# A spectral and dense layer stack on one core: rows turned through memory by SyncE, filter ordering on VectorE, evacuations assigned by phase

## The chip, the cores and the metric

The kernel runs on one core of a Trainium2 chip. The engines of a core that matter here are TensorE (PE, matrix products, with its weight loads shown apart as PEld), VectorE (DVE), ScalarE (ACT), GpSimd (POOL) and SyncE (SP). Each works through its own instructions in order, and they wait for one another by semaphores. SP, POOL and ACT also issue DMAs; a DMA waits on the engine that issues it, so whatever stands behind it on that engine waits too. Matrix products land in PSUM, eight banks of 128 partitions, from which DVE or ACT must carry them to the on-chip memory ("evacuate" them); the kernel hands out the banks in four pairs, in turn.

The metric is the device time of one execution in microseconds (us). A number such as L549 is a line of the kernel before.

## The reference

Four layers in a row on x of 2048 rows and 1024 columns, in bfloat16: twice a spectral layer A and a dense layer B.

```python
def _A_ref(x, w_r, w_i):
    X = rfft2(x.astype(float32), axes=(-2, -1))
    X = X * (w_r + 1j * w_i)
    return irfft2(X, s=(S, D), axes=(-2, -1)).astype(bfloat16)

def _B_ref(x, w1, b1, w2):
    h = einsum("bsd,df->bsf", x, w1) + b1
    sp = log1p(exp(-abs(h))) + where(h > 0, h, 0)
    return einsum("bsf,fd->bsd", h * tanh(sp), w2)

x = x + _A_ref(_layernorm(x), A_w_r, A_w_i)
x = x + _B_ref(_layernorm(x), B_w1, B_b1, B_w2)
x = x + _A_ref(_layernorm(x), A_w_r, A_w_i)
x = x + _B_ref(_layernorm(x), B_w1, B_b1, B_w2)
```

F, the hidden width of B, is 3584.

## The kernel before

**Layer A.** The two-dimensional transform and its inverse are products with tables of cosines and sines, in five stages. The first, `s1`, is a short transform along 16 row blocks and 8 column blocks: 128 products of a 128x128 slice of XR (x in another order) with a small matrix, eight of them to a PSUM pair, sixteen pairs j. In the first layer A the normalisation is folded into that small matrix: `scaled(j)` makes eight scaled copies MN of the table M0 (128x128 each), shared out among POOL, DVE and ACT, and `s1` asks for them four pairs ahead. In the second layer A the input is normalised already, one fixed M serves for all, and no copies are made.

The rest is cut into eight groups g and run as a software pipeline of twelve steps in `layer_A`: in step k, two halves each, `s2` of group k (L642), in the first layer A also `filter_bins` of group k (L834), `s3` of group k-1 (L680 to L683), `i1` of group k-3 (L709), `i2` of group k-4 (L730, L748). Each has its evacuation: L670 or L672 for `s2`, L687 for `s3`, L716 for `i1`, L756 or L758 for `i2`. After `s3` DVE multiplies by the complex filter WT with four instructions (L691 to L698). `filter_bins` brings the filter into the order of the bins: TensorE mirrors a part of it (L834), ACT writes that part (L848), and four plain copies with a stride of eight elements move the rest (L842, L845), on POOL in the first layer A. `keep_filter` does the same once more during the first layer B, with the copies on DVE, and stores the ordered filter in memory (`w_scratch`), from where the second layer A loads it.

**The turn.** The result U of a group has 16 rows of interest, each spread over 128 partitions, and the last product `i4` (L875) needs them turned: UT with row and group on the partitions. `row` moves one such row with one DMA from on-chip memory to on-chip memory, 128 pieces of 256 bytes into one partition. For groups 0 to 5 rows 0 to 7 go that way, all issued by SP; rows 8 to 15 go through memory, a write to `u_scratch` issued by SP and, a step later, `u_back` issued by POOL. Of groups 6 and 7 all rows go by `row`, on SP, POOL and ACT. `i4` waits for the whole of UT, and so does everything in layer B.

**Layer B.** Products with W1 (L930), Mish on ACT (L934), products with W2 (L948), added to x by DVE (L953). The weights stream in on SP.

The order on each engine is the order in which the program's methods are called; there is no scheduler. Two places matter beyond that. `constants` is called before `s1`, and in it POOL converts a small bias table (L399), which waits for the last of a row of loads that SP issues. And `u_turn` has a small table that names the queue of each row of groups 6 and 7.

Of the kernel before, what the change touches and what calls it, by code (L numbers as in the profile page):

```python
# [6 lines left out]
ALU = mybir.AluOpType  # L7
P = 128
BF = dt.bfloat16
# [165 lines left out]
class KB:  # L175
# [120 lines left out]
    def build(self):  # L296
# [5 lines left out]
        self.u_d = nc.dram_tensor("u_scratch", (8, P, 8, P), BF, kind="Internal").ap()  # L302
# [237 lines left out]
    def scaled(self, j):  # L540
        rt = self.RT
        rc = rt.ap.rearrange("p a b -> p (a b)")
        for q in range(8):
            n = 8 * j + q
            if q % 4 == 1:
                self.op(self.act, lambda e, n=n: e.activation(self.MN.ap[:, n, :], self.M0.ap, ACT.Copy, scale=rc[:, n:n + 1]),
                        reads=[rt.res, self.M0.res], parts=[self.r_mn[j]])
            else:
                self.op(self.pool if q % 8 in (2, 4, 7) else self.dve, lambda e, n=n: e.tensor_scalar(self.MN.ap[:, n, :], self.M0.ap, rc[:, n:n + 1], None, op0=ALU.mult),  # L549
                        reads=[rt.res, self.M0.res], parts=[self.r_mn[j]])  # L550

    def s1(self, li):
# [60 lines left out]
    def layer_A(self, li):  # L613
# [20 lines left out]
        def s2(g, half):  # L634

            ps, banks, _ = self.pair()
            y = self.Y.ap
            at = lambda r: y[:, r * 8 + g, :]
            fns = []

            def mm(dst, r, t, start, stop):
                fns.append(lambda e: e.matmul(dst, at(r), FD[:, t:t + dst.shape[-1] * 2], start=start, stop=stop))  # L642
            for i in range(2):
                d = ps[:, i * 512:(i + 1) * 512].rearrange("p (r k) -> p r k", r=2)
                if half == 0:
                    for kd in range(2):
                        for c in range(2):
                            mm(d[:, :, kd * P:(kd + 1) * P], 4 * kd + 2 * c + i, kd * 512 + c * 256, c == 0, c == 1)
                    continue
                for c in range(2):  # L650
                    mm(d[:, :, 0:P], 8 + 4 * c + i, 1024 + c * 256, c == 0, c == 1)
                for kd in range(2):
                    dd = d[:, :, P + kd * 64:P + kd * 64 + 64]
                    r, t = 10 + 4 * kd, (3 + kd) * 512
                    if g == 0:
                        mm(dd, r + i, t, True, True)
                    else:
                        for c in range(2):
                            mm(dd, r + c, t + c * 256 + i * P, c == 0, c == 1)
            self.group(fns, reads=[self.Y.res, self.r_fd], writes=banks)  # L660
            za, zb = zslot(g, 0), zslot(g, 1)

            zz = self.ARENA[:, o["Z"] // 2 + (2 * g % 6) * K:o["Z"] // 2 + (2 * g % 6 + 2) * K].rearrange(
                "p (s r k) -> p s r k", s=2, r=2)
            if half == 0:
                za.res.begin()
                zb.res.begin()
            dst, src = zz[:, :, :, 256 * half:256 * half + 256], ps.rearrange("p (s r k) -> p s r k", s=2, r=2)
            if half == 0:
                self.op(act, lambda e: e.activation(dst, src, ACT.Copy), reads=banks, parts=[za.res, zb.res])  # L670
            else:
                self.op(dve, lambda e: e.tensor_copy(dst, src), reads=banks, parts=[za.res, zb.res])  # L672
# [45 lines left out]
        def i2(g, half):  # L718
# [33 lines left out]
            if half == 0:  # L752
                u.res.begin()
            dst = u.ap[:, 8 * half:8 * half + 8, :].rearrange("p a b -> p (a b)")
            if half == 0 and g % 2 == 0:
                self.op(dve, lambda e: e.tensor_copy(dst, ps), reads=banks, parts=[u.res])  # L756
            else:
                self.op(act, lambda e: e.activation(dst, ps, ACT.Copy), reads=banks, parts=[u.res])  # L758
# [6 lines left out]
        def u_turn(g, half):  # L765

            u = U[g % 3]
            if half and g < 6:
                self.dma(sp, self.u_d[g], u.ap[:, 8:16, :], f"uw{g % 3}", reads=[u.res], writes=[self.r_ud[g]])
                return  # L770
            order = {6: (sp, pool), 7: ((sp, pool, sp, pool, sp, pool, sp, pool), (act, sp, act, act, sp, act, sp, act))}
            who = order[g][half] if g in order else sp
            for i in range(8):
                row(who[i] if isinstance(who, tuple) else who, g, 8 * half + i)
# [50 lines left out]
    def filter_bins(self, g, ps, banks, wr, wts, jt, r_jt, eng):  # L825

        fns = []
        for i in range(2):
            src, j0 = (i, (2, 0)[i]) if g == 0 else (1 - i, 0)
            for c in range(2):  # L830
                for kd in (1, 2, 3):
# [2 lines left out]
                    fns.append(lambda e, col=col, j=(j0 + c) * P, mov=mov: e.matmul(  # L834
                        ps[:, col:col + 64], jt[:, j:j + P], mov, start=True, stop=True))
        self.group(fns, reads=[wr.res, r_jt], writes=banks)
        for i in range(2):
            wt = wts[i]
            wt.res.begin()
            d3 = wt.ap[:, :, 0:384].rearrange("p c (k i) -> p c k i", i=P)  # L840
            lo = wr.ap[:, :, i, :].rearrange("p c (i k) -> p c k i", k=8)
            self.op(eng, lambda e, d3=d3, lo=lo: e.tensor_copy(d3[:, :, :, 0:64], lo[:, :, 0:3, :]),  # L842
                    reads=[wr.res], parts=[wt.res])
            dd = wt.ap[:, :, 384:512].rearrange("p c (k i) -> p c k i", i=64)
            self.op(eng, lambda e, dd=dd, lo=lo: e.tensor_copy(dd, lo[:, :, 3:8:4, :]),  # L845
                    reads=[wr.res], parts=[wt.res])
            src = ps[:, 512 * i:512 * i + 384].rearrange("p (c k i) -> p c k i", c=2, i=64)
            self.op(self.act, lambda e, d3=d3, src=src: e.activation(d3[:, :, :, 64:128], src, ACT.Copy),  # L848
                    reads=banks, parts=[wt.res])

    def keep_filter(self, g):

# [8 lines left out]
        self.filter_bins(g, self.PS[:, 6:8, :].rearrange("p a b -> p (a b)"), self.r_bank[6:8], wr, ws, jt.ap, jt.res, self.dve)  # L861
# [237 lines left out]
```

## Time and profile before

| What | us |
|---|---|
| Median of three runs (1150.26 to 1158.82) | 1154.47 |
| The profiled execution, of which all lines here are | 1154.65 |
| its span in the trace | 1152.8 |
| TensorE busy / DVE / ACT / POOL | 986.0 / 377.2 / 335.1 / 149.0 |
| first layer A: start to first product of `s2` | 0 to 80.72 |
| first layer A: the pipeline, to the end of the last evacuation | 80.72 to 166.39 |
| wait for UT until `i4` | 166.39 to 185.53 |
| first layer B until `s1` of the second layer A | 185.53 to 634.75 |
| second layer A: `s1` and pipeline, to the last evacuation | 634.75 to 712.34 |
| wait for UT until `i4` | 712.34 to 730.30 |
| second layer B | 730.30 to 1152.8 |

The rows of a profile are read so. In a timeline a row has its start, its length, the engine, the line, what is written from what, the shape and how often; brackets hold the engine's idle time just before and what ended it. In the groups by line, after the bar: the busy time, the mean ns of one, and the idle time before them with what ended it. In the table by stretch of time each engine has its busy time and its count, then the granted TensorE clock (1.00 is full speed), the share of the DMA engines and GB/s. The chain of waits goes back from the last instruction to whatever released it, and so shows what the end hung on; "issue" in it is time in which the engine waited for nothing that the profile names. The layers B, 870 us of the span, are TensorE work almost without gaps; the change concerns the two layers A and a part of `filter_bins` that runs within layer B.

### The profile page before, as it was taken

Reading aid. Unit: us, or ns where it says so; the run is one execution under the profiler, and the core shown is the slowest. Engines: PE = TensorE matmul, PEld = TensorE weight load, DVE = VectorE, ACT = ScalarE, POOL = GpSimd, SP = SyncE. Lnnn points to the kernel's source line nnn. Section 1 sums busy time; section 2 is a strip of 40 time slices with the busy share of each in tenths; the row PEclk is TensorE's granted clock in tenths of the full one; section 3 lists DMA queues with packets and bytes.
Section 4 is the critical chain, followed back from the end, with each engine's and each line's share of the span. In section 5 each row is a group of like instructions: output and inputs, shape, how many; then the busy total and the mean of one; then the engine's idle time right before and its main releaser. Section 6 shows DMA issues by size and latency. Waiting matters only on the chain.

```text
span 1152.8 us, 14555 instructions
## 1 busy us (share of the span) xinstructions
PE 986.0 (86%) x6090; PEld 522.3 (45%) x6185; DVE 377.2 (33%) x795; ACT 335.1 (29%) x466; POOL 149.0 (13%) x219
## 2 busy tenths in 40 slices
PE   0167973899999999999995795499999999999998
PEld 0145753444444445544442674344444444444443
DVE  6158844551044421102442783555101110000011
ACT  6045762434300024430000685243320003432000
POOL 1287531000000002200031022100000000000000
PEclk9999995999999999999998998599999999999999
DMA  9503567144400015522095057614440002210000
GB/s 282 122 4 106 123 128 152 38 151 160 147 19 19 19 55 183 183 91 74 23 116 72 29 165 135 134 48 136 146 147 19 28 19 62 76 55 1 28 19 28
DMA packets 128449, 101.97 MB, mean 88 GB/s; under 512 B 48000, under 2 KB 105600, under 8 KB 128384
## 3 DMA queue, kind: packets, MB, share of 16 engines
q1 hardware_dynamic: 114832, 69.37, 21.5%
q0 software_dynamic: 11680, 31.25, 11.8%
q10 hardware_dynamic: 1872, 0.43, 0.5%
q8 instruction: 49, 0.80, 0.3%
q14 instruction: 16, 0.13, 0.0%
HBM read 79.93 MB, written 15.47 MB: 83 GB/s over the span
## 4 chain that ended last, share of the span: by engine, by line
PE 70%; DVE 9%; DMA 8%; issue 5%; POOL 4%; ACT 3%; SPq 1%; ACTq 0%; POOLq 0%; DVEq 0%
PE PS L948 33%; PE PS L930 28%; DMA ARENA<-in_A_w_i_dram 3%; POOL ARENA L549 2%; DMA u_scratch<-ARENA 2%; DMA ARENA<-ARENA 2%; POOL ARENA L242 1%; PE PS L642 1%; DVE BN L431 1%; PE PS L912 1%; DVE XS L881 1%; PE PS L834 1%; DMA XS<-in_A_x_dram 1%; PE PS L709 1%; PE PS L730 1%
## 5 line engine op out<-in xcount | busy, mean ns | idle before, releaser
L930 PE MATMUL PS<-ARENA 128*128 128x512 bf16 x1750 | 389.3, 381 | 5.8 <-DVE ARENA L917 2.2
L948 PE MATMUL PS<-ARENA 128*128 128x512 bf16 x1754 | 387.4, 379 | 2.0
L934 ACT ACTIVATE ARENA<-PS,B 128x512 bf16<-128x512 f32 x224 | 153.8, 688 | 438.6 <-PE PS L930 438.5
L930 PEld LDWEIGHTS PS<-ARENA 128*128 128x128 bf16 x1792 | 175.5, 98 | 213.0 <-issue 4.5
L948 PEld LDWEIGHTS PS<-ARENA 128*128 128x128 bf16 x1792 | 174.7, 98 | 207.6
L953 DVE TENSOR_TENSOR XS<-PS,XS 128x512 bf16<-128x512 f32 x64 | 44.3, 692 | 502.3 <-PE PS L948 502.3
L431 DVE BATCH_NORM_STATS2 BN<-XS 128x6 f32<-128x512 bf16 x108 | 69.6, 674 | 7.6 <-DMA XS<-in_A_x_dram 6.4
L875 PE MATMUL PS<-MT,ARENA 128*128 128x32 bf16 (+1 forms) x768 | 24.5, 187 | 47.9 <-DMA ARENA<-ARENA 39.6
L881 DVE TENSOR_TENSOR XS<-PS,XS 128x512 bf16<-128x512 f32 (+1 forms) x40 | 29.1, 790 | 96.1 <-PE PS L875 96.1
L570 ACT ACTIVATE ARENA<-PS 128x1024 bf16<-128x1024 f32 x16 | 16.3, 1024 | 149.8 <-PE PS L564 149.5
L564 PE MATMUL PS<-ARENA 128*128 128x128 bf16 x128 | 16.2, 306 | 38.4 <-POOL ARENA L549 33.5
L875 PEld LDWEIGHTS PS<-MT,ARENA 128*128 128x128 bf16 x768 | 22.9, 100 | 51.4 <-issue 44.7
L687 ACT ACTIVATE ARENA<-PS 128x1024 bf16<-128x1024 f32 x32 | 32.7, 1023 | 25.8 <-PE PS L683 25.8
L412 ACT ACTIVATE ARENA<-XS 128x1024 bf16<-128x1024 bf16 x20 | 21.1, 1056 | 59.5 <-DVE XS L881 48.5
L642 PE MATMUL PS<-FD,ARENA 128*128 128x256 bf16 (+1 forms) x312 | 35.5, 266 | 2.7 <-DVE ARENA L572 1.2
L709 PE MATMUL PS<-ARENA 128*128 128x256 bf16 x256 | 34.1, 277 | 2.3 <-DMA ARENA<-c_bt 2.3
L242 POOL DMA_DIRECT2D w_scratch<-ARENA x8 | 4.6, 576 | 230.9 <-ACT ARENA L848 230.9
L572 DVE CAST ARENA<-PS 128x1024 bf16<-128x1024 f32 x16 | 19.1, 1222 | 45.4 <-PE PS L564 45.4
L716 ACT ACTIVATE ARENA<-PS 128x1024 bf16<-128x1024 f32 x32 | 32.6, 1020 | 4.4 <-PE PS L709 4.4
L642 PEld LDWEIGHTS PS<-FD,ARENA 128*128 128x128 bf16 x312 | 27.6, 103 | 9.3 <-issue 1.9
L691 DVE TENSOR_TENSOR ARENA<-ARENA 128x1024 bf16<-128x1024 bf16 x32 | 25.4, 794 | 18.7 <-ACT ARENA L687 18.6
L564 PEld LDWEIGHTS PS<-ARENA 128*128 128x128 bf16 x128 | 12.4, 138 | 42.2 <-issue 39.1
(72 smaller groups left out, 689.6 us busy)
## 6 DMA issues: line engine op xcount, KB each, us to landing
ARENA<-in_B_w_dram SPq DMA_DIRECT2D x56, 512.0 KB, 4.0
ARENA<-in_B_w_dram SPq DMA_DIRECT2D x56, 256.0 KB, 4.3
ARENA<-ARENA SPq DMA_DIRECT2D x129, 32.0 KB, 3.9
XS<-in_A_x_dram SPq DMA_DIRECT2D x4, 1024.0 KB, 8.8
ARENA<-in_A_x_dram SPq DMA_DIRECT2D x32, 128.0 KB, 3.2
ARENA<-in_A_w_r_dram POOLq DMA_DIRECT2D x16, 256.0 KB, 4.2
ARENA<-in_A_w_i_dram POOLq DMA_DIRECT2D x16, 256.0 KB, 4.2
w_scratch<-ARENA POOLq DMA_DIRECT2D x8, 512.0 KB, 2.9
```

Of the source, the lines that this page charges most:

```text
L431: self.op(self.dve, lambda e: e.bn_stats(self.BN[:, j, 6 * h:6 * h + 6], self.XS[:, j, 512 * h:512 * h + 512]), reads=[self.r_xs[j]], part ...
L564: fns.append(lambda e, q=q, n=n, ps=ps, m=m: e.matmul(ps[:, q * P:(q + 1) * P], XR.ap[:, n, :], m, start=True, stop=True))
L642: fns.append(lambda e: e.matmul(dst, at(r), FD[:, t:t + dst.shape[-1] * 2], start=start, stop=stop))
L687: self.op(act, lambda e: e.activation(x.ap.rearrange("p a b -> p (a b)"), ps, ACT.Copy, scale=SIG), reads=banks, writes=[x.res])
L709: fns.append(lambda e, c=c, part=part: e.matmul(ps[:, c * 256:(c + 1) * 256], yk.ap[:, part, c * P:(c + 1) * P], t[:, (128, 0)[part]:(384, ...
L716: self.op(act, lambda e: e.activation(v.ap[:, :, i, :], src, ACT.Copy), reads=banks, parts=[v.res])
L875: fns.append(lambda e, l=l: e.matmul(ps[:, w * l:w * l + w], self.UT.ap[:, u0 + l, :], self.MT[:, 8 * lo:8 * lo + w], start=True, stop=True))
L881: self.op(self.dve, lambda e: e.tensor_tensor(xs, src, xs, ALU.add), reads=rb, parts=self.r_xs[lo:lo + nb])
L930: fns.append(lambda e, db=db, bank=bank, fl=fl: e.matmul(PS[:, bank, :], wb.ap[:, db, fl * P:(fl + 1) * P], x.ap[:, db, :], start=(db == 0 ...
L934: self.op(act, lambda e, bank=bank, ft=ft: e.activation(at.ap[:, ft, :], PS[:, bank, :], ACT.Mish, bias=self.B1[:, ft:ft + 1]), reads=[sel ...
L948: fns.append(lambda e, i=i, ft=ft: e.matmul(PS[:, bank, :], at.ap[:, ft, t * P:(t + 1) * P], W2[ft].ap[:, h * 512:(h + 1) * 512], start=(i ...
L953: self.op(dve, lambda e: e.tensor_tensor(xs, PS[:, bank, :], xs, ALU.add), reads=[self.r_bank[bank]], writes=[self.r_xs[j]])
```

## The change

It has four parts.

- `scaled`: POOL no longer makes copies MN. Of eight, ACT makes two, DVE six instead of three.
- `filter_bins`: in the first layer A the plain copies move from POOL to DVE, and everywhere two instructions do what four did: one copies 4 of the 8 strided components of both slots and both parts (1024 elements a partition), one a fifth component (256). ACT's two stay.
- Evacuations: the second half of `s2` goes to ACT instead of DVE for groups 0 to 2. For `i2`, DVE takes both halves of groups 5 to 7, and in the second layer A also the first half of groups 1 and 3; before it took the first half of groups 0, 2, 4 and 6.
- The turn: for groups 0 to 5 all 16 rows go through memory (`u_scratch` is twice as large: 512 KB written, 512 KB read back by each), and both the write and `u_back` are issued by SP. The rows of groups 6 and 7 alternate between SP and POOL, with ACT in the last half of group 7.

```diff
-            if q % 4 == 1:
+            if q % 3 == 2:
                 self.op(self.act, ... self.MN.ap[:, n, :] ...)
             else:
-                self.op(self.pool if q % 8 in (2, 4, 7) else self.dve, ... self.MN.ap[:, n, :] ...)
+                self.op(self.dve, ... self.MN.ap[:, n, :] ...)
...
-            self.filter_bins(g, ps, banks, self.WR[g % 2], WT[2 * g % 8:2 * g % 8 + 2], self.JT, self.r_jt, pool)
+            self.filter_bins(g, ps, banks, self.WR[g % 2], WT[2 * g % 8:2 * g % 8 + 2], o["WT"] + 2048 * (2 * g % 8),
+                             self.JT, self.r_jt, dve)
...
-            if half == 0:
+            if half == 0 or g < 3:
                 self.op(act, ... s2 ...)
...
-            if half == 0 and g % 2 == 0:
+            if g > 4 or (half == 0 and g % 2 and li):
                 self.op(dve, ... i2 ...)
...
             u = U[g % 3]
-            if half and g < 6:
-                self.dma(sp, self.u_d[g], u.ap[:, 8:16, :], f"uw{g % 3}", reads=[u.res], writes=[self.r_ud[g]])
+            if g < 6:
+                if half:
+                    self.dma(sp, self.u_d[g], u.ap, f"uw{g % 3}", reads=[u.res], writes=[self.r_ud[g]])
                 return
-            order = {6: (sp, pool), 7: ((sp, pool, sp, pool, sp, pool, sp, pool), (act, sp, act, act, sp, act, sp, act))}
...
+            order = {6: ((sp, pool) * 4,) * 2, 7: ((sp, pool) * 4, (act, sp, pool, act, sp, act, sp, act))}
...
         def u_back(g):
-            self.dma(pool, self.UT.ap[64 + g:P:8, :, :], self.u_d[g].rearrange("l r n -> r l n"), f"um{g % 3}",
+            self.dma(sp, self.UT.ap[g:P:8, :, :], self.u_d[g].rearrange("l r n -> r l n"), f"um{g % 3}",
                      reads=[self.r_ud[g]], parts=[self.UT.res])
...
+        for k, n, col in ((0, 4, 0), (7, 1, 448)):
+            dst = both[:, :, :, col:512].rearrange("p s c (k i) -> p s c k i", k=n)[:, :, :, :, 0:64]
+            src = own[:, :, :, k:k + n, :]
+            self.op(eng, lambda e, dst=dst, src=src: e.tensor_copy(dst, src), reads=[wr.res], parts=parts)
         for i in range(2):
...
-            self.op(eng, lambda e, d3=d3, lo=lo: e.tensor_copy(d3[:, :, :, 0:64], lo[:, :, 0:3, :]),
-                    reads=[wr.res], parts=[wt.res])
...
-            self.op(eng, lambda e, dd=dd, lo=lo: e.tensor_copy(dd, lo[:, :, 3:8:4, :]),
-                    reads=[wr.res], parts=[wt.res])
```

How the rows of two engines change at the two places on which most depends. In these rows stand the line, the operation, what is written from what, the shape, and how often in a row. Lines of the changed kernel are up to three higher than before.

At the opening, POOL, from the last table load ahead of `s1` into the pipeline. Before:

```order
L242 DMA ARENA<-c_bt 128x768
L399 CAST B<-B1h 128x28
L549 ISA
L549 TENSOR_SCALAR ARENA<-ARENA 128x128 x48
L842 COPY ARENA<-ARENA 128x2x3x64
L845 COPY ARENA<-ARENA 128x2x128
```

and now:

```order
L242 DMA ARENA<-c_bt 128x768
L399 CAST B<-B1h 128x28
L242 DMA ARENA<-in_A_w_r_dram 128x2x512
L242 DMA ARENA<-in_A_w_i_dram 128x2x512
L242 DMA ARENA<-c_ft 128x768
```

The 48 scalings and the filter copies have left POOL, and its next instruction after the bias table is a load for the pipeline.

At the same place DVE, from the end of `s1` (L549 are the scalings, L572 the evacuations) to the first multiplies. Before:

```order
L572 CAST ARENA<-PS 128x128x8
L549 TENSOR_SCALAR ARENA<-ARENA 128x128 x6
L572 CAST ARENA<-PS 128x128x8 x2
L672 CAST ARENA<-PS 128x4x256
L691 TENSOR_TENSOR ARENA<-ARENA 128x1024
L693 TENSOR_TENSOR ARENA<-ARENA 128x1024
```

and now:

```order
L572 CAST ARENA<-PS 128x128x8
L549 TENSOR_SCALAR ARENA<-ARENA 128x128 x12
L572 CAST ARENA<-PS 128x128x8 x2
L847 COPY ARENA<-ARENA 128x16x64
L847 COPY ARENA<-ARENA 128x4x64
```

Between two evacuations stand twelve scalings where six stood, and ahead of the first multiplies the filter copies of group 0 (and then of group 1), where the evacuation of `s2` stood.

At the end of each layer A, SP, from the write of group 4 to the first weights of layer B. Before (the plain ARENA<-ARENA rows are `row`):

```order
L242 DMA u_scratch<-ARENA 128x1024
L242 DMA ARENA<-ARENA 1x128x128 x8
L242 DMA u_scratch<-ARENA 128x1024
L242 DMA ARENA<-ARENA 1x128x128 x15
L242 DMA ARENA<-in_B_w_dram 128x8x256 x4
```

and now, from the write of group 5:

```order
L242 DMA u_scratch<-ARENA 128x2048
L242 DMA ARENA<-u_scratch 16x128x128
L242 DMA ARENA<-ARENA 1x128x128 x8
L242 DMA ARENA<-u_scratch 16x128x128
L242 DMA ARENA<-ARENA 1x128x128 x7
L242 DMA ARENA<-in_B_w_dram 128x8x256 x4
```

The eight rows of each of the groups 0 to 5 are gone from SP; the read-backs stand there instead, the last one between the rows of group 6 and those of group 7.

POOL at the same place, before:

```order
L242 DMA ARENA<-c_bt 128x768
L242 DMA ARENA<-u_scratch 8x128x128 x2
L242 DMA ARENA<-ARENA 1x128x128 x8
L242 DMA ARENA<-u_scratch 8x128x128
L242 DMA ARENA<-ARENA 1x128x128 x4
```

and now:

```order
L242 DMA ARENA<-c_bt 128x768
L242 DMA ARENA<-c_ft 128x768
L242 DMA ARENA<-c_bt 128x768 x3
L242 DMA ARENA<-ARENA 1x128x128 x13
L242 DMA ARENA<-c_jt 128x512
```

No read-back stands on POOL any more, neither between the loads of tables nor ahead of the rows.

More of the change, by code (lines that the diff above doesn't have):

```diff
@@ L823, in load_wr, with filter_bins @@
                      reads=[self.r_xs[15]] if g < 2 else [])
-    def filter_bins(self, g, ps, banks, wr, wts, jt, r_jt, eng):
+    def filter_bins(self, g, ps, banks, wr, wts, off, jt, r_jt, eng):
+        both = self.ARENA[:, off // 2:off // 2 + 2048]
         fns = []
@@ L836, in filter_bins @@
         self.group(fns, reads=[wr.res, r_jt], writes=banks)
-        for i in range(2):
[L838 to L842, printed above, removed]
-                    reads=[wr.res], parts=[wt.res])
-            dd = wt.ap[:, :, 384:512].rearrange("p c (k i) -> p c k i", i=64)
-            self.op(eng, lambda e, dd=dd, lo=lo: e.tensor_copy(dd, lo[:, :, 3:8:4, :]),
-                    reads=[wr.res], parts=[wt.res])
+        for w in wts:
+            w.res.begin()
+        parts = [w.res for w in wts]
+        both = both.rearrange("p (s c k) -> p s c k", s=2, c=2)
+        own = wr.ap.rearrange("p c s (i k) -> p s c k i", k=8)
+        for k, n, col in ((0, 4, 0), (7, 1, 448)):
+            dst = both[:, :, :, col:512].rearrange("p s c (k i) -> p s c k i", k=n)[:, :, :, :, 0:64]
+            src = own[:, :, :, k:k + n, :]
+            self.op(eng, lambda e, dst=dst, src=src: e.tensor_copy(dst, src), reads=[wr.res], parts=parts)
+        for i in range(2):
             src = ps[:, 512 * i:512 * i + 384].rearrange("p (c k i) -> p c k i", c=2, i=64)
+            d3 = both[:, i, :, 0:384].rearrange("p c (k i) -> p c k i", i=P)
             self.op(self.act, lambda e, d3=d3, src=src: e.activation(d3[:, :, :, 64:128], src, ACT.Copy),
-                    reads=banks, parts=[wt.res])
+                    reads=banks, parts=parts)
     def keep_filter(self, g):
```

9 lines of the change are left out of this document (4 added, 5 removed).

## The prediction

> **What bounds the kernel now.** I read the page first, then the chain of waits, then each stage by stretches of time.
>
> ```profile
> span 1152.8 us, 14555 instructions
> PE 986.0 (86%) x6090; PEld 522.3 (45%) x6185; DVE 377.2 (33%) x795; ACT 335.1 (29%) x466; POOL 149.0 (13%) x219
> ```
>
> TensorE is busy for 986.0 of 1152.8 us. What the change can win lies in the rest, and the chain of waits (start, length, what) says where that is:
>
> ```profile
> 19.73 29.89 issue
> ...
> 50.52 27.90 POOL ARENA L549 x47
> ...
> 166.82 8.67 DMA u_scratch<-ARENA
> ...
> 178.48 6.48 DMA ARENA<-ARENA
> ...
> 712.11 8.99 DMA u_scratch<-ARENA
> ...
> 724.21 5.63 DMA ARENA<-ARENA
> ```
>
> Three stretches stand out: some 58 us in the opening, in which POOL first waits and then scales tables, and two waits at the ends of the layers A, each for a write to memory and then for rows. Between them lie the two pipelines, by stretch of time:
>
> ```profile
> 82.00:168.00 86.00, 73.54 (x647) 56.10 (x653) 61.79 (x76) 57.59 (x68) 46.36 (x60) 0.94 0.46 112
> 646.00:712.00 66.00, 57.75 (x557) 43.13 (x564) 46.13 (x77) 49.77 (x52) 14.24 (x22) 1.00 0.48 125
> ```
>
> No engine is full in either; TensorE (first busy figure) comes nearest, and the first layer's clock is 0.94 where the second has 1.00. These five places make the sum.
>
> **The opening.** The timelines of POOL, DVE, ACT and PE, then the loads of XR on SP (first the durations of their issue, min/median/max, then the landing of the last ones), and FD's landing:
>
> ```profile
> 49.64 0.21 POOL L399 CAST B<-B1h 128x28 f32<-128x28 bf16 x1 [29.91 <-DMA B1h<-in_B_b_dram]
> 49.91 28.50 POOL L549 TENSOR_SCALAR ARENA<-ARENA 128x128 bf16<-128x128 bf16 x48
> 25.42 2.04 DVE L549 TENSOR_SCALAR ARENA<-ARENA 128x128 bf16<-128x128 bf16 x12
> 57.52 1.33 DVE L549 TENSOR_SCALAR ARENA<-ARENA 128x128 bf16<-128x128 bf16 x6
> 639.15 6.88 DVE L572 CAST ARENA<-PS 128x1024 bf16<-128x1024 f32 x6 [0.42 <-PE PS L564]
> 25.42 3.03 ACT L546 ACTIVATE ARENA<-ARENA 128x128 bf16<-128x128 bf16 x10 [4.52 <-DVE ARENA L532]
> 80.72 1.87 PE L642 MATMUL PS<-FD,ARENA 128*128 128x256 bf16 x8 [1.16 <-issue]
> L242 SPq DMA_DIRECT2D ARENA<-in_A_x_dram x32: 627/628/3161, 7.1 to 38.5; - x32
> DMA to landing us min/median/max: 3.1/3.6/4.1
> FD<-c_fd SPq DMA_DIRECT2D x1, 640.0 KB, 6.0
> ```
>
> DVE and ACT had the scales at 25.42 and made their first copies at once. POOL stood behind the bias table until 49.64, and then needed 28.50 us for its 48 copies. The change removes both: nothing of `s1` is on POOL any more, and the wait for the bias table holds back nothing that `s1` needs. What is late next? DVE, with 96 copies and 8 evacuations. With POOL idle a copy takes 2.04/12 = 0.17 us, an evacuation 6.88/6 = 1.15 us: 16.3 + 9.2 = 25.5 us, from 25.42 to 51. ACT's 32 copies (0.30 each) and 8 evacuations fit beside that. XR's last load is issued at 38.5 and lands 4.1 later, at 42.6, for the last quarter of `s1` alone, which DVE reaches later; FD, issued behind it, lands at about 45. So `s2` starts at about 51 instead of 80.72: 29.7 us less. One end is the loads: 42.6 and some 6 us for the last four pairs, 48.5, a gain of 32. The other is DVE at the copy price beside a busy POOL, 1.33/6 = 0.22 us: 55.7, a gain of 25. POOL does nothing beside it then, so I take the first price.
>
> **The first pipeline.** The multiplies in the first layer A and in the second; then the same filter copies on DVE in layer B; then the idle time of PE by releaser (in all, times, longest), three rows of the first layer and three of the second; last, one group of L834:
>
> ```profile
> L693 DVE TENSOR_TENSOR ARENA<-ARENA 128x1024 bf16<-128x1024 bf16 x16 | 16.4, 1023 | 0.0
> L693 DVE TENSOR_TENSOR ARENA<-ARENA 128x1024 bf16<-128x1024 bf16 x16 | 10.9, 684 | 0.0
> L842 DVE COPY ARENA<-ARENA 128x384 bf16<-128x384 bf16 x16 | 7.9, 497 | 68.5 <-DMA ARENA<-in_A_w_i_dram 68.5
> L845 DVE COPY ARENA<-ARENA 128x256 bf16<-128x256 bf16 x16 | 6.1, 380 | 0.0
> ...
> PE PS L680 <- DVE ARENA L672: 4.0, 2, 3.2
> PE PS L834 <- DVE ARENA L672: 2.8, 1, 2.8
> PE PS L730 <- DVE ARENA L756: 1.5, 1, 1.5
> ...
> PE PS L681 <- DVE ARENA L672: 2.7, 2, 2.0
> PE PS L709 <- DMA ARENA<-c_bt: 2.3, 1, 2.3
> PE PS L680 <- DVE ARENA L672: 1.8, 1, 1.8
> ...
> 124.19 1.37 PE PS L834 x12
> ```
>
> The multiply takes 1023 ns in the first layer and 684 in the second, where POOL copies nothing. PE waits there 8.3 us for evacuations that stand behind such multiplies on DVE, and its mean clock is 0.94. The change takes POOL's copies out of their way and gives DVE copies of its own: from 497 ns for 384 elements and 380 for 256, about 0.91 ns an element, so 1024 elements take 1.08 us, and with the short one 1.46 us a group, 11.7 in all. That is less than the stretch that goes, by the whole of DVE's account: it is busy 61.79 us in this pipeline and 46.13 in the second, which has the same multiplies, 15.7 less. With the 11.7 DVE comes to 58 of some 76, still below TensorE. Three evacuations of `s2` leave DVE at the steps where PE waits, and ACT has room. To size it I take the second layer as it stands, 66, add eight L834 groups, 11, take off the c_bt wait, 2.3, and two thirds of its DVE waits, 3; I add 4 for a start at a cut clock and for DVE's new copies in the first steps. That is about 76, against 85.7 now (80.72 to the last evacuation below): 10 less. Ends: 14 less (all waits and the clock), and none.
>
> The copies in layer B shrink from 1.75 to 1.46 us a group and hide under the products of L930; I count nothing (0 to 2.4, eight times 0.3).
>
> **The second pipeline.** u_back no longer stands on POOL ahead of the loads of BT: the 2.3 us go. The L672 waits, 4.5, go for groups 0 to 2, but ACT then carries four evacuations a step there, so I keep a part: 5 us less in all, between 0 and 6.8. ACT gives back more `i2` evacuations than it takes.
>
> **The turn, twice.** Last evacuations of each layer, SP's rows, a write of 512 KB, the read-backs as POOL issued them:
>
> ```profile
> 164.45 1.94 ACT L758 ACTIVATE ARENA<-PS 128x1024 bf16<-128x1024 f32 x2 [0.54 <-DMA u_scratch<-ARENA]
> 185.53 4.62 PE L875 MATMUL PS<-MT,ARENA 128*128 128x32 bf16 x172 [20.57 <-DMA ARENA<-ARENA]
> ...
> 710.37 1.97 ACT L758 ACTIVATE ARENA<-PS 128x1024 bf16<-128x1024 f32 x2 [0.22 <-PE PS L730]
> 730.30 4.86 PE L875 MATMUL PS<-MT,ARENA 128*128 128x32 bf16 x178 [19.02 <-DMA ARENA<-ARENA]
> ...
> 167.51 10.59 SPq L242 DMA_DIRECT2D ARENA<-ARENA  x15
> ...
> ARENA<-ARENA SPq DMA_DIRECT2D x129, 32.0 KB, 3.9
> w_scratch<-ARENA POOLq DMA_DIRECT2D x8, 512.0 KB, 2.9
> ARENA<-u_scratch POOLq DMA_DIRECT2D x12, 256.0 KB, 7.0
> ...
> 131.04 1.10 POOL L242 DMA_DIRECT2D ARENA<-u_scratch  x1 [2.89 <-DMA u_scratch<-ARENA]
> ```
>
> From the last evacuation (166.39 and 712.34) to `i4` pass 19.1 and 18.0 us. SP is late with the rows of group 5, so the write of that group is issued at 166.82 and lands 8.67 later; POOL's read-back waits for it, and four rows of group 7 stand behind that. Now a group costs SP one write and one read-back instead of eight rows (0.7 us each) and a write, and the write goes out as soon as its data is there. The read-back is new on SP. It has 2048 pieces of 256 bytes from memory; XR's loads are the same with 512, issued in 0.63 us each, 3.16 at worst: between 0.63, if issue does not grow with pieces, and 12.6, four times the worst. I take 1.6, since most XR loads stand at the low end, and keep both ends. SP is free for group 6 some 3 us before the last evacuation; eight rows 5.6, the read-back 1.6, seven rows 4.9, and a landing of 3.9 make 16, that is 13 us after it. What waits behind the read-back are the rows of group 7; its own write (2.9 us) has long landed. So 6.3 and 5.2 us less; ends 9 us after the evacuation, and no gain.
>
> Here the Trainium skill speaks against the change: "DMA: Bandwidth & Descriptors", section "Why small descriptors are slow (HBM only)", says that small pieces cost extra with main memory and not between on-chip memories. By that rule the old rows are the better path, and the sum would be that of the second rival. The XR rows do not bear it out: 512 pieces go out in 0.63 us, about as fast as the 128 of a row (0.7).
>
> **The sum.** 29.7 + 10 + 5 + 6.3 + 5.2 = 56.2, from the profiled 1154.65 (span 1152.8), which is 0.2 above the median of the runs: 1098.
>
> **Rivals.** First: DVE becomes the bound of both pipelines. Its copies are in order ahead of the multiplies and can wait for filter loads. For it: DVE had 61.79 busy of 86. Against it: the 684 ns price. No gain in either pipeline: 1098 + 15 = 1113.
> Second: the read-back is slow. POOL's takes 7.0 us for 256 KB; at twice that for 512 KB and issued 4 us after the last evacuation, it lands at 18, and the turns gain next to nothing: 1098 + 11 = 1109.
> Third, the other side: issue of the read-back blocks SP at up to 12.6 us. The first one comes 35 us before the last evacuation (131.04); six, 15 rows and a landing end at 6 x 12.6 - 35 + 14.5 = 55 us after it, 42 later than I forecast, twice: 1182. It decides from about 10 us apiece (28 later in each turn). Against it: only the XR loads in the crowded first microseconds took so long.
> Fourth: the opening does not do what it says, because XR or DVE at the contended price sets its end: 1103, up to 1110 if both pipelines lose a little too.
>
> **How the numbers follow.** Forecast 0.60, first rival 0.15, second 0.13, fourth 0.08, third 0.04. The forecast alone spans 1083 (32 + 14 + 6.8 + 10 + 9 = 72 less) to about 1108. The range must take in the first, second and fourth: 1083 to 1120; the third and mixtures of two rivals are left out. About 1% is what a measurement of this kernel can tell from no change. All but the third are faster by more; the third splits by its price: faster 0.95, same 0.02, slower 0.03.
>
> **What would show it.** Opening: no L549 on POOL, first `s2` product near 51. First pipeline: L693 near 684 ns, PE clock near 1.00, some 76 us. Turn: `i4` about 13 us after the last evacuation, SP issuing a read-back in 1 to 2.5 us. Wrong would make it: `s2` after 56, PE waiting for DVE copies, or SP held for several us by a read-back.

## The result and the profile after

| | us |
|---|---|
| the changed kernel, median of four runs (1100.71 to 1105.14) | 1103.36 |
| the kernel before, median of four (1150.01 to 1158.82) | 1152.37 |
| ratio, with its 95% interval | 0.956 (0.952 to 0.961) |
| the profiled execution / its span | 1102.66 / 1100.8 |

The change makes the kernel 4.4% faster. By stages, each read as in the table of before (first product of `s2`, end of the last evacuation, first product of `i4`); the last column is the term of the prediction:

| stage | before | after | difference | forecast |
|---|---|---|---|---|
| start to `s2`, first layer A | 80.72 | 50.32 | -30.4 | -29.7 |
| first pipeline | 85.67 | 73.94 | -11.7 | -10 |
| first turn | 19.14 | 15.79 | -3.3 | -6.3 |
| layer B and `s1` of the second layer A | 460.56 | 459.65 | -0.9 | 0 |
| second pipeline | 66.25 | 61.47 | -4.8 | -5 |
| second turn | 17.96 | 17.12 | -0.9 | -5.2 |
| second layer B | 422.50 | 422.51 | 0 | 0 |
| span | 1152.8 | 1100.8 | -52.0 | -56.2 |

Everything but the two turns came out within 2 us of its term. The page of the changed kernel first:

```profile
span 1100.8 us, 14504 instructions
PE 985.6 (90%) x6185; PEld 521.0 (47%) x6185; DVE 377.1 (34%) x843; ACT 333.4 (30%) x466; POOL 81.0 (7%) x129
```

TensorE does the same work, 985.6 us against 986.0. POOL is busy 68 us less (81.0 against 149.0), and DVE, which took that work over, is no busier than before (377.1 against 377.2), mainly because its own multiplies became shorter.

The opening, in the timelines of DVE, POOL and PE (start, length, engine, line):

```profile
25.51 3.99 DVE L549 TENSOR_SCALAR ARENA<-ARENA 128x128 bf16<-128x128 bf16 x24
...
30.55 2.03 DVE L549 TENSOR_SCALAR ARENA<-ARENA 128x128 bf16<-128x128 bf16 x12
...
47.91 2.35 DVE L572 CAST ARENA<-PS 128x1024 bf16<-128x1024 f32 x2
...
50.03 0.21 POOL L399 CAST B<-B1h 128x28 f32<-128x28 bf16 x1 [30.31 <-DMA B1h<-in_B_b_dram]
...
50.32 0.61 PE L643 MATMUL PS<-FD,ARENA 128*128 128x256 bf16 x2 [1.23 <-DVE ARENA L572]
```

DVE works almost without a gap from 25.51, twelve copies in 2.03 us (0.17 apiece) between evacuations, and `s2` waits for its last evacuation, 0.7 us from the forecast 51. POOL still waits for the bias table, until 50.03, but nothing that `s1` needs stands behind it any more.

The two pipelines by stretch of time, then DVE's groups in the first one (after the bar: busy time, mean ns of one, idle time before):

```profile
51.00:124.00 73.00, 70.80 (x658) 55.53 (x656) 54.70 (x91) 57.81 (x69) 18.85 (x31) 0.95 0.59 158
...
600.00:661.00 61.00, 57.73 (x563) 43.02 (x561) 47.23 (x77) 48.39 (x51) 11.76 (x23) 1.00 0.61 168
```

```profile
L694 DVE TENSOR_TENSOR ARENA<-ARENA 128x1024 bf16<-128x1024 bf16 x16 | 10.9, 684 | 0.0
L847 DVE COPY ARENA<-ARENA 128x1024 bf16<-128x1024 bf16 x8 | 8.6, 1079 | 0.0
...
L847 DVE COPY ARENA<-ARENA 128x256 bf16<-128x256 bf16 x8 | 3.1, 388 | 0.0
```

The multiply (L693 before, L694 now) takes 684 ns, the copies 1079 and 388 ns, as sized from the second layer and from layer B. TensorE is busy 70.80 of 73 us: it bounds this pipeline now, and its waits for DVE's evacuations, 8.3 us before, are down to one:

```profile
PE PS L836 <- DVE ARENA L673: 0.9, 1, 0.9
```

The turn is where the forecast missed. Timelines of the end of the first layer A, and of the second:

```profile
120.12 6.59 SPq L242 DMA_DIRECT2D ARENA<-ARENA  x8
...
120.74 3.52 DVE L757 CAST ARENA<-PS 128x1024 bf16<-128x1024 f32 x3 [0.64 <-PE PS L749]
...
126.75 0.60 SPq L242 DMA_DIRECT2D ARENA<-u_scratch  x1
127.40 10.28 SPq L242 DMA_DIRECT2D ARENA<-ARENA  x7
...
140.05 4.79 PE L878 MATMUL PS<-MT,ARENA 128*128 128x32 bf16 x178 [17.19 <-DMA ARENA<-ARENA]
...
678.29 0.88 PE L878 MATMUL PS<-MT,ARENA 128*128 128x32 bf16 x27 [18.52 <-DMA ARENA<-ARENA]
```

The last evacuation ends at 124.26. SP issues the last read-back in 0.60 us, but then its seven rows take 10.28 us. The instructions on SP around that place, with the issue time of one in ns and, below, the time from issue to landing:

```profile
L242 SPq DMA_DIRECT2D ARENA<-u_scratch x1: 601/601/601, 126.8 to 126.8; - x1
L242 SPq DMA_DIRECT2D ARENA<-ARENA x1: 6417/6417/6417, 127.4 to 127.4; - x1
...
DMA to landing us min/median/max: 8.8/9.9/11.0
```

One row, the first behind the read-back, holds SP for 6.4 us, and the read-back lands 11.0 us after its issue, where over the whole kernel its median is half of that:

```profile
ARENA<-u_scratch SPq DMA_DIRECT2D x12, 512.0 KB, 5.3
```

The second layer A repeats it. The chain of waits, which ran through a write and a row there before, now runs along SP's issues, with one that stands still and the landing of the last row:

```profile
665.32 6.63 SPq L242
...
675.21 2.79 DMA ARENA<-ARENA
```

### The profile page after: what moved, and what is told of

Read it like the earlier page. It is cut to its first block, busy times and chain, and to the rows that moved or that the text cites. A ratio compares the mean times of both kernels' runs of the same rounds, so it can differ in the third digit from the quotient of the medians.

```text
span 1100.8 us, 14504 instructions
## 1 busy us (share of the span) xinstructions
PE 985.6 (90%) x6185; PEld 521.0 (47%) x6185; DVE 377.1 (34%) x843; ACT 333.4 (30%) x466; POOL 81.0 (7%) x129
## 5 line engine op out<-in xcount | busy, mean ns | idle before, releaser
L933 PEld LDWEIGHTS PS<-ARENA 128*128 128x128 bf16 x1792 | 175.0, 98 | 211.7 <-issue 2.2
L951 PEld LDWEIGHTS PS<-ARENA 128*128 128x128 bf16 x1792 | 174.7, 98 | 207.7
L847 DVE COPY ARENA<-ARENA 128x1024 bf16<-128x1024 bf16 (+1 forms) x32 | 21.9, 730 | 69.6 <-DMA ARENA<-in_A_w_i_dram 61.9
L692 DVE TENSOR_TENSOR ARENA<-ARENA 128x1024 bf16<-128x1024 bf16 x32 | 22.1, 689 | 25.8 <-ACT ARENA L688 20.5
L915 PE MATMUL PS<-IDENT,ARENA 128*128 128x128 bf16 x256 | 21.4, 241 | 9.6 <-DVE ARENA L474 7.1
L710 PEld LDWEIGHTS PS<-ARENA 128*128 128x128 bf16 x256 | 25.1, 99 | 8.9 <-issue 0.3
L836 PE MATMUL PS<-ARENA 128*128 128x64 bf16 x192 | 24.8, 293 | 4.1 <-DMA ARENA<-in_A_w_i_dram 3.1
```

The lines of the kernel that those rows point to most:

```text
L710: fns.append(lambda e, c=c, part=part: e.matmul(ps[:, c * 256:(c + 1) * 256], yk.ap[:, part, c * P:(c + 1) * P], t[:, (128, 0)[part]:(384, ...
L915: fns.append(lambda e, db=db: e.transpose(PSb[:, bank, db * P:(db + 1) * P], xn.ap[:, db * P:(db + 1) * P], self.IDENT[:]))
L933: fns.append(lambda e, db=db, bank=bank, fl=fl: e.matmul(PS[:, bank, :], wb.ap[:, db, fl * P:(fl + 1) * P], x.ap[:, db, :], start=(db == 0 ...
L951: fns.append(lambda e, i=i, ft=ft: e.matmul(PS[:, bank, :], at.ap[:, ft, t * P:(t + 1) * P], W2[ft].ap[:, h * 512:(h + 1) * 512], start=(i ...
```

## The experiments

Two questions were open: whether the four gains are separate and due to what the prediction names, and what holds up the turn. Each time stands beside one of the kernel before on the same chip. Where no rounds are named, it is a single run, and runs of one kernel differ by some us (1150.01 to 1158.82 for the kernel before), so it is the stages that decide and not the totals.

**The opening alone** (before, with the new sharing of the copies MN only; 1122.06 us, kernel before 1157.59):

```diff
-            if q % 4 == 1:
+            if q % 3 == 2:
                 self.op(self.act, ...)
             else:
-                self.op(self.pool if q % 8 in (2, 4, 7) else self.dve, ...)
+                self.op(self.dve, ...)
```

> The kernel before with only the sharing of the MN copies changed (ACT 2 of 8, DVE 6, POOL none). Theory, the opening stands by itself: first s2 product at 50 to 51 us as in the changed kernel (80.7 before), pipeline and turns as before (about 86 and 19 us), so 30 us less than before, about 1123. Rival, the gain in the opening needs the filter copies off POOL as well, or is handed back by the pipeline: s2 at 50 but the pipeline longer than 90, less than 22 us in all.

`s2` begins at 50.28 us and the span, 1120.2 us, is 32.6 shorter than that of the profiled kernel before; the pipeline behind it stays at 86.0. The gain of the opening is carried to the end in full, and it is independent of the rest.

**Only the wait goes** (before, with POOL's conversion of the bias table put behind `s1`; POOL keeps its 48 copies; 1132.57 us, kernel before 1157.59):

```diff
-        self.op(self.pool, lambda e: e.tensor_copy(self.B1[:], self.B1h[:]), ...)
+        self.r_b1h = r
...
         self.s1(li)
...
+        if li == 0:
+            self.op(self.pool, lambda e: e.tensor_copy(self.B1[:], self.B1h[:]), ...)
```

> The kernel before with one instruction moved: POOL converts the bias table after s1 instead of ahead of it; the MN copies stay shared as before. Theory, most of the opening's loss was POOL standing behind the bias table: POOL starts its 48 copies at about 25.4 and, at 0.6 us each, ends at 54; first s2 product at 55 to 57 instead of 80.7, about 24 us less than before, near 1130, and 5 to 6 us more than with DVE. Rival, POOL's slow copies were the loss and the wait was covered by XR's loads: s2 after 65, less than 16 us gained.

POOL's copies and the first `s2` product of this kernel:

```profile
25.38 28.73 POOL L549 TENSOR_SCALAR ARENA<-ARENA 128x128 bf16<-128x128 bf16 x48 [5.88 <-DVE ARENA L532]
...
56.42 0.80 PE L642 MATMUL PS<-FD,ARENA 128*128 128x256 bf16 x3 [1.16 <-issue]
```

POOL needs 28.7 us, as before (28.5), but begins 24 us earlier, and `s2` comes 24.3 us earlier. So of the 30 us, 24 were the wait behind the bias table, and 6 POOL's slowness. Moving one small conversion would have bought four fifths.

**The turn alone** (before, with the turn's part of the diff; 1149.81 us, kernel before 1157.59). The edit is the three pieces of the diff from `u = U[g % 3]` to `u_back`, and the larger `u_scratch`.

> The kernel before with only the turn changed (groups 0 to 5 whole through memory, both DMAs on SP, the new queues for the rows of groups 6 and 7). Theory, what the changed kernel shows is due to the turn alone: from the last evacuation to i4 about 16 and 17 us (19.1 and 18.0 before), the wait for BT's table in the second pipeline (2.3 us) gone, about 6 us less in all, near 1148; a row behind the last read-back takes 6 us to issue. Rival, the turn's waits depend on the evacuations' engines: turns unlike those by more than 2 us.

The turns take 16.50 and 17.80 us. The second pipeline is 2.3 us shorter, the wait of PE for the table BT gone from the list: that small term of the prediction was right. The first pipeline is 2.2 us longer here (87.87), at a granted clock of 0.92 instead of 0.94; why is open.

**The last read-back on another queue** (the changed kernel; 1106.60 us, kernel before 1157.59). If SP's blocked issue was the cost, the rows must gain:

```diff
-            self.dma(sp, self.UT.ap[g:P:8, :, :], ...)
+            self.dma(act if g == 5 else sp, self.UT.ap[g:P:8, :, :], ...)
```

> The changed kernel with only the read-back of group 5 issued by ACT instead of SP. In the changed kernel the row of group 7 that stands behind that read-back on SP takes 6.4 and 6.6 us to issue, the others 0.6. Theory, the read-back fills SP's queue: now all 15 rows issue in 0.6 us each, SP ends its rows 5 to 6 us earlier, and i4 starts 4 to 5 us earlier in each turn (11 to 12 us after the last evacuation), 8 to 10 us less in all, near 1093. Rival, the DMA engines themselves are full of 256-byte pieces at that point, whoever issues them: rows issue sooner but land later, i4 moves by less than 1.5 us in each turn, about 1101.

SP's rows in this kernel, and how long they took to land:

```profile
L242 SPq DMA_DIRECT2D ARENA<-ARENA x15: 599/601/2037, 120.2 to 131.0; - x15
...
DMA to landing us min/median/max: 5.9/9.5/11.7
```

SP is rid of the stall: its 15 rows go out one after the other, the last at 131.0 instead of 137. But they land 9.5 us after their issue in the median, up to 11.7, and `i4` starts at 140.33 instead of 140.05. In the second layer A the turn even takes 19.22 us instead of 17.12. ACT's rows there, and the first `i4` product:

```profile
L242 ACTq DMA_DIRECT2D ARENA<-ARENA x4: 627/686/5218, 663.0 to 669.7; - x4
...
682.19 1.97 PE L878 MATMUL PS<-MT,ARENA 128*128 128x32 bf16 x68 [20.63 <-DMA ARENA<-ARENA]
```

The stall has moved along with the read-back: the row behind it now holds ACT, for 2.97 us in the first turn and 5.22 in the second. The blocked issue is a sign of the jam and not its cause; my first theory, SP's queue, fell here. The Trainium skill, "DMA: Bandwidth & Descriptors", section "Issuing engines are not separate DMA queues", says that DMAs issued from several engines end on the same 16 DMA engines and that another queue saves only the time to issue; the trace agrees, with a last issue 6 us earlier and an end 0.3 later in the first turn.

**Two parts of the pipelines.** The changed kernel with the old rule for the evacuations (1106.63 us), and with the filter copies of the first layer A on POOL in the new form of two instructions (1115.32 us); the kernel before took 1153.91 beside both.

```diff
-            if half == 0 or g < 3:
+            if half == 0:
...
-            if g > 4 or (half == 0 and g % 2 and li):
+            if half == 0 and g % 2 == 0:
```

> The changed kernel with the evacuations on the engines of before (second half of s2 always on DVE; of i2 DVE takes the first half of groups 0, 2, 4, 6). Theory, the new assignment removes PE's waits for L672 in the first steps: without it the second pipeline takes 64 to 66 us instead of 61.5 and the first 76 to 78 instead of 73.9, 5 to 8 us more in all. Rival, it is worth nothing here, since the waits go elsewhere: both pipelines within 1 us.

The pipelines become 1.8 and 2.4 us longer (75.72 and 63.91), 4.2 in all where 5 to 8 were expected; the rival, at most 1 us each, is refuted. The second figure and the 2.3 us of BT make up the 4.8 of the second pipeline.

```diff
-                             self.JT, self.r_jt, dve)
+                             self.JT, self.r_jt, pool)
```

> The changed kernel with the filter copies of the first layer A on POOL, in the new form of two instructions. Theory, POOL's copies stretch DVE's multiplies: L694 near 1000 ns instead of 684 in the first layer, PE waiting for DVE, the first pipeline 80 to 84 us instead of 73.9. Rival, the copies cost DVE as much as the stretch did: the first pipeline within 2 us of 73.9.

The first pipeline takes 87.20 us, 13.3 more and more than I had expected. DVE's multiply in this kernel, and what PE waits for in its first pipeline:

```profile
L694 DVE TENSOR_TENSOR ARENA<-ARENA 128x1024 bf16<-128x1024 bf16 x16 | 15.3, 955 | 0.0
```

```profile
PE PS L836 <- DVE ARENA L673: 6.8, 1, 6.8
PE PS L643 <- DVE ARENA L673: 5.2, 2, 4.4
```

With POOL copying, the same multiply needs 955 ns in the mean instead of 684, and PE waits 12.0 us for evacuations behind such multiplies, where it waited 0.9. The mean hides two kinds: the median is 0.69 us, and a multiply that meets POOL's copies takes up to 3.27, about as long as they do:

```profile
69.64 3.27 DVE L694 TENSOR_TENSOR ARENA<-ARENA 128x1024 bf16<-128x1024 bf16 x1
```

```profile
70.31 3.08 POOL L847 COPY ARENA<-ARENA 128x1024 bf16<-128x1024 bf16 x2
```

That is the mechanism of the prediction, and it carries 11 of the 13 us. Work taken over by DVE cost less than the same work beside DVE. The two parts do not add up one by one: 13.3 and 1.8 are more than the 11.7 of the whole, and with POOL copying the new evacuations give nothing (87.20 against 85.67 in the kernel before).

**Fewer rows.** If not the queue, then the rows themselves: each asks for 128 pieces of 256 bytes that end in one partition. So groups 6 and 7, too, went through memory on SP, and no rows were left (1087.31 us, kernel before 1153.91); then group 6 alone, its read-back on ACT (1100.70 us, same chip).

```diff
-            if g < 6:
+            if g < 8:
                 if half:
                     self.dma(sp, self.u_d[g], u.ap, ...)
...
-            if 0 <= g5 - 1 < 6:
+            if 0 <= g5 - 1 < 8:
                 u_back(g5 - 1)
+            if g5 == 7:
+                u_back(7)
```

> The changed kernel with groups 6 and 7 turned through memory too, write and read-back on SP; no rows at all. Theory, what makes the turn long is the rows and the read-back competing in SP's queue: alone, a write lands in 3.2 and a read-back in 5.3 us, so i4 starts 9 to 11 us after the last evacuation instead of 15.8 and 17.1, 12 to 14 us less in all, near 1089. Rival, read-backs close behind one another are what is slow (7.7, 10.4 and 11 us to landing at the end of the changed kernel): group 7's lands 10 us or more after its issue, i4 14 us or more after the last evacuation, under 5 us gained.

> The changed kernel with group 6 turned through memory too and its read-back issued by ACT; group 7 by rows as it stands. Theory of SP's queue: rows of group 7 issue in 0.6 us each, the read-back of group 6 lands about 8 us after the last evacuation, i4 at 10 to 12 us after it, 9 to 12 us less in all. Rival, the DMA engines are full: i4 at 14 us or later.

Without rows the turns take 10.36 and 10.07 us, with one group of rows 13.70 and 13.73. The first is what the theory said, though SP's queue, the reason it gave, had fallen with the run before; the second lies close to the 14 of the rival and not in the 10 to 12 of SP's queue. SP and the first `i4` product in the kernel without rows:

```profile
124.47 1.75 SPq L242 DMA_DIRECT2D u_scratch<-ARENA  x1
...
126.39 3.78 SPq L242 DMA_DIRECT2D ARENA<-u_scratch  x2
...
134.80 1.36 PE L880 MATMUL PS<-MT,ARENA 128*128 128x32 bf16 x45 [11.76 <-DMA ARENA<-u_scratch]
```

What is left is a write and a read-back, one after the other. Now the DMA engines just behind the last evacuation, by stretch of time (the last two columns are their busy share and GB/s; a share above 1 means that transfers overlap on an engine). The changed kernel, then the one without rows:

```profile
124.00:130.00 6.00, 0.00 (x0) 0.00 (x0) 0.26 (x1) 0.00 (x0) 3.30 (x7) 0.66 1.33 94
```

```profile
124.00:130.00 6.00, 0.00 (x0) 0.00 (x0) 0.44 (x1) 0.00 (x0) 0.00 (x0) 0.71 1.04 293
```

Both are full. But with rows the engines move 94 GB/s, and without them 293. Half of the 293 is writes, which go out in pieces of 4 KB (128x2048 bf16). While only read-backs run, in pieces of 256 bytes, it is still twice what it is with rows, 198 GB/s:

```profile
130.50:133.50 3.00, 0.00 (x0) 0.00 (x0) 0.00 (x0) 0.00 (x0) 0.00 (x0) 0.50 1.05 198
```

**More rows, and the same kernels with more rounds.** Groups 5, 6 and 7 by rows (1107.17 us, one run); the kernel without rows in five rounds; the changed kernel beside it in five rounds.

```diff
-            if g < 6:
+            if g < 5:
...
-            order = {6: ((sp, pool) * 4,) * 2, ...
+            order = {5: ((sp, pool) * 4,) * 2, 6: ((sp, pool) * 4,) * 2, ...
...
-            if 0 <= g5 - 1 < 6:
+            if 0 <= g5 - 1 < 5:
```

> The changed kernel with one more group by rows: groups 5, 6 and 7 go by rows (48 of them, on SP, POOL and ACT), groups 0 to 4 through memory. Theory (each row costs the DMA engines, about 2.5 to 3.5 us a group, as with 0, 1 and 2 groups of rows: about 10.2, 13.7 and 16.5 us a turn): the turns become 18.5 to 20.5 us, the time 1107 to 1111 us. Rival (the last read-back, issued 6 us before the last evacuation and landing 11 us later, is what holds the rows of groups 6 and 7 up; a kernel whose read-backs are all done by then has shorter turns): the turns become 13 to 15 us, the time 1096 to 1100 us.

> The kernel with all eight groups through memory on SP and no rows, in five rounds. Theory: 1087 us, a ratio to the kernel before of 0.942 to 0.945, and 14 to 17 us below the changed kernel on the same chip; both turns 10 to 10.5 us. Rival (the single look was a lucky one): within 5 us of the changed kernel.

> The changed kernel as it is, beside the kernel without rows and the kernel before on one chip. Theory: 1101 to 1105 us, ratio to the kernel before 0.955 to 0.958, turns 15.5 to 16.5 and 16.5 to 17.8 us. Rival (turns scatter from run to run by more than the 2 us that the change gives them): a turn below 14 or above 19 us.

| groups by rows | first turn, us | second turn, us |
|---|---|---|
| 0 (two runs) | 10.36, 10.54 | 10.07, 10.06 |
| 1 | 13.70 | 13.73 |
| 2 (the change, two runs) | 15.79, 16.54 | 17.12, 16.83 |
| 3 | 20.81 | 18.72 |

Each group of rows adds about 3 us, from none to three: (20.81 - 10.45) / 3 = 3.5 and (18.72 - 10.07) / 3 = 2.9. The rival, that a late whole read-back holds the rows up, is not tested by this run, since its last read-back, group 4's, stands behind eight rows on SP and is late too:

```profile
L242 SPq DMA_DIRECT2D ARENA<-u_scratch x1: 599/599/599, 122.7 to 122.7; - x1
...
DMA to landing us min/median/max: 17.9/17.9/17.9
```

It is issued 0.6 us before the last evacuation, and among the rows of three groups it needs 17.9 us to land. The next experiment speaks against that rival: its last whole read-back lands at about 128, and its rows are slow after that.

In five rounds on one chip the kernel without rows takes 1089.22 us (median of four runs), a ratio to the kernel before (1152.76) of 0.9446 (0.9426 to 0.9465); the changed kernel takes 1104.60, 0.9579 (0.9562 to 0.9596). Leaving out the rows is worth another 15 us, and that version is faster than both.

**Which end of a row is slow?** All eight groups through memory, but the read-backs of groups 6 and 7 cut into 16 transfers each, one row of UT apiece (1107.24 us, kernel before 1151.72):

```diff
         def u_back(g):
+            if g > 5:
+                for r in range(16):
+                    q = (sp, pool, act)[r % 3]
+                    self.dma(q, self.UT.ap[r * 8 + g:r * 8 + g + 1, :, :],
+                             self.u_d[g][:, r:r + 1, :].rearrange("l r n -> r l n"), ...)
+                return
```

> The kernel with all eight groups through memory, but the read-backs of groups 6 and 7 cut into 16 transfers each, one row of UT apiece, in turn on SP, POOL and ACT: the same 128 pieces of 256 bytes into one partition as a row had, with main memory as the source instead of 128 partitions. It tells apart why rows are slow. If it is their source (128 partitions of on-chip memory): the turns stay near those of one read-back a group, 11 to 12.5 us (SP has some 10 of the 32 to issue at 0.6 us after the last write, and the last lands 3 us after it), the time 1088 to 1093 us. If it is their end (one partition, one transfer a row): each group costs 2.5 to 3.5 us more, as rows do, the turns 15.5 to 17 us, the time 1098 to 1103 us.

The turns take 16.96 and 21.14 us; the first is what was expected of one-partition ends, the second is beyond both expectations, and why it is so long is open. In the first one, by stretch of time, and by the DMA issues from 118 to 145 us (KB of one, median us to landing):

```profile
130.00:136.00 6.00, 0.00 (x0) 0.00 (x0) 0.00 (x0) 0.00 (x0) 2.53 (x5) 0.50 1.40 98
```

```profile
ARENA<-u_scratch SPq DMA_DIRECT2D x2, 512.0 KB, 5.6
ARENA<-u_scratch SPq DMA_DIRECT2D x12, 32.0 KB, 7.5
```

The same pieces from the same memory: sixteen rows in one transfer (groups 4 and 5, issued ahead of the cut ones) land in 5.6 us, one row by itself, among the others, in 7.5, and the engines are as full (1.40) and as slow (98 GB/s) as with rows from on-chip memory. So it is not the source, nor a late whole read-back, for none was under way then. It is that a transfer ends in a single partition, or that there are 32 transfers instead of two, on three queues instead of one; these change together here, and which of them counts stays open. For the first speaks the Trainium skill, "SBUF — State Buffer", section "Door 1: The DMA port swizzle": DMA bandwidth depends on how many of the 16 ports the partitions of a transfer reach. One row reaches one port; no run here varies the number of ports by itself. By the 435 GB/s for all ports that the Trainium skill's page "DMA: Bandwidth & Descriptors" gives in the section "Where 436 GB/s comes from", a port would have 27 GB/s, an estimate from that page, and three queues with one row each under way at a time some 80. The two stretches above show 94 and 98, which is more, and no run shows how many rows a queue has under way.

## Why the prediction was right, and where it was off

- **The opening** was right in mechanism and size: 30.4 against 29.7, with DVE's 0.17 us a copy as the clock of it. The second run showed which part weighs what. The fourth rival, an opening that ends later, is refuted by `s2` at 50.32.
- **The first pipeline** came to 73.94 us where the sum said 76. Multiplies and copies have the forecast durations. The 4 us that I added for the cut clock and for DVE's new copies was too much: the mean clock is 0.95 and not near 1.00 as forecast, but PE waits only 0.9 us for DVE. The first rival, DVE as the bound, is refuted by its 54.70 busy of 73 us.
- **The second pipeline**: 4.8 against 5, made up of 2.3 (BT) and 2.4 (evacuations).
- **The two turns** are the step that failed: "eight rows 5.6, the read-back 1.6, seven rows 4.9, and a landing of 3.9 make 16, that is 13 us after it". It measured 15.8 and 17.1 after it, and 16.5 and 17.8 with the turn's part alone. The gain is 4.2 us where 11.5 were forecast, and hardly more than the scatter of the old turn (16.7 to 20.9 and 16.9 to 18.0 in the kernel before and the first two experiments). Term by term, the eight rows took 6.6, the read-back 0.6, the seven rows 10.3 and the landing 2.4: the seven rows are the one mis-sized, by the one that stood still for 6.4 us. But a better price for it would not have mended the sum. With the stall taken away from SP, the landing grew to 9.5, and the end stayed in the first turn and came 2.1 later in the second. What failed is that the time was summed from SP's issues: the DMA engines, filled by rows, set it.
- **The second rival**, a read-back that is slow and leaves the turns without gain (1109), was nearer to the size of the gain (4.2 us, where it said next to nothing) and had the place wrong. The last read-back does land 13.5 us after the last evacuation (126.75 + 11.0 - 124.26), where the rival said 18. But read-backs are slow only in the company of rows; between whole writes and read-backs one lands in 5 to 6 us (5.1 for the last one of the first turn without rows).
- **The third rival**, SP blocked by the read-back, was seen in part, once in each turn, at 6.4 and 6.6 us, and cost nothing of its own: with SP freed of it the rows did not land sooner.
- **The rule on small pieces**, weighed in the prediction, points the other way from these runs. By the Trainium skill, "DMA: Bandwidth & Descriptors", section "Why small descriptors are slow (HBM only)", the old rows should be the better path. Here a group is turned faster through main memory, read back in the same pieces of 256 bytes, and rows read from main memory run at 98 GB/s where those from on-chip memory run at 94. Also, the reason for doubt that I gave, the issue times of XR, was not the one that counts: rows go out as fast as read-backs, in 0.6 us, and it is their landing, one row at a time, that is slow.

In the total the turns' miss of 7.3 us is by chance partly offset by 1.7 and 0.7 more in the first pipeline and the opening, and 0.9 in layer B: 1098 became 1102.66 in the profiled run.

## What to carry to other kernels

Price a burst of DMAs at the end of a stage by what the DMA engines move, and not by the issue times of its queue; a landing time taken over the whole kernel does not hold in a burst. Turn rows with one transfer that spreads over many partitions, through memory if need be, and cut the number of one-row transfers first. Before work is moved from one engine to another, look at what the slow one waits for: a wait of a small conversion ahead of the work was worth four times the difference between the engines.

## What the runs showed of the hardware that was not expected

- A path over main memory, write and read-back in turn, 10.1 to 10.5 us for the last 512 KB, beats 16 rows from on-chip memory to on-chip memory, which need no second step (13.7 with one such group).
- An issue on SP stood still for 6.4 and 6.6 us behind a transfer of 2048 pieces while the DMA engines were full; with the read-back moved to ACT, the row behind it held ACT for 2.97 and 5.22 us.
- Busy DMA engines say little: at a share of 1.0 to 1.4 they moved 293 GB/s with whole writes and read-backs, 198 with read-backs alone, and 94 to 98 with rows.
- A DVE multiply of 0.68 us that met POOL's two copies of a group took 3.27 us, about as long as they did (3.08).
